# Keeping the last two chunks of h in SBUF, forming four more weight operands in place, and accumulating a product onto a PSUM copy of another

## The chip, the cores and the metric

One core of one Trainium2 chip runs the kernel. The metric is device time in microseconds of one launch. Of the kernel before, three runs are given. The profile is that of one more execution of the same program.

## What is computed

The reference adds two sublayers under a gate (batch 1, sequence S = 2048, D = 512, F = 1376, all float32):

```python
g = sigmoid((x * gate_w).sum(-1, keepdims=True))
a = x @ dft_hid_re.T ; b = x @ dft_hid_im.T
y = dft_seq_re @ a - dft_seq_im @ b          # Fourier mixing
h = silu(x @ w1) * (x @ w3)
out = g * y + (1 - g) * (h @ w2)
```

## The kernel before

**Arithmetic.** Every float32 operand of a matrix product is split into a high half, rounded to the type that TensorE takes (fp32r), and a low half, the rest. A product is then three matmuls (high by high, high by low, low by high), written by `mm3` (L79). `split` (L70) makes the halves: ScalarE copies the source into the high half (L71), VectorE subtracts that from the source for the low half (L74). On top of this every large product is computed by Strassen's scheme in Winograd's form: seven products of quarter blocks, P1 to P7, of operands that are first summed ("forms"), and sums of products in place of the eighth.

**Stages.** First come the hidden-dimension DFT (tiles `dP`, L190 to 240), whose result `ab` goes to DRAM, then the eleven column chunks c = 0 to 10 of h (`item`, L413; tiles `X`, `Y`, `Z`, `Yi`), and then the steps of the six output blocks (`step`, L847; tiles `P`, in the last third also `Lx`). Block b = (m, j): m = 0 is h @ w2, m = 1 and 2 are the two sequence DFTs, j is a half of the sequence. A step is one product (P1 ... P7) with one quarter q of its contraction: 12 matmuls, 6 where the quarter is half as wide. TensorE takes all of this in one stream.

**Order of the work.** The program is written in the order of the stages; a planner that simulates the engines at build time then orders each engine's instructions by priority, which is the order of the program, among what it takes to be ready. Each engine runs its list strictly in that order, so an instruction whose data are late holds back all that stand behind it on its engine. `keep_in_program_order` (called `pinned` in places) ties an instruction behind the one written before it on its engine; loads of the step stage are tied so (`fetch`, L580). DMAs are issued by SyncE (loads) and GpSimd (stores, and adds in DRAM). In the step stage `advance(n)` (L706) issues at step n the loads for step n + 8, the operand sums (L669) for step n + 4 and the halves for step n + 3.

**Buffers.** SBUF tiles come from pools with a fixed number of buffers: `f4` (19, float32 sources and results), `op` (28, operands that stay) and `zo` (8, halves that are used soon). A tile waits for a buffer that has fallen free. PSUM is held as four pairs of banks, `pp0` to `pp3`.

**h.** In `item`, `u2` and `u4` of chunk c end as two tiles of h, 128x1024 each; `store_h` (L409) writes them to DRAM: chunk 10 to `hpl`, the others to `hsp`. The first two output blocks (m = 0) load them again in `load_c` (L649), in pairs of chunks (q = 0, 1, 2; q = 2 is the single chunk 4 or 9), and chunk 10 in `load_plain` (L713), where the products with the last rows of w2 (the steps with q "pl") take it.

**Forms of the weights.** `forms(m, q, ks, keep)` (L473) loads two sources `r` from DRAM (L481), makes the sums `m..` (L490 to 501, L77), splits them, and either stores the halves to `fsp` (L514) or, with `keep`, leaves them in SBUF. The list `later` (L942 to 951) holds the forms made during the chunks, and `work` takes them off one by one, six for each chunk. For m = 1 the forms of P1, P5, P6 and P3 are made there for q = 0, 1, 2 and loaded again by `load_a`; those of q = 3 are made in place, two steps apart, from the third step of block 1 on (L1045 to 1049). The last entries of `later` are `inner_forms` (L530), which store to `lsp`.

**The end of a product.** At the last step of P1, P5 and P6, ScalarE copies the accumulated pair `whole` from PSUM to an `f4` tile (L904 to 906). P2 has a pair of its own; at its end VectorE adds it to the copy of P1 (L911), and `finish` (L779) scales by the gate, or stores.

**First chunks.** Before the loop over the chunks `first1(0)` and the parts of `second(0, n)` run in the order 0, 3, 1, 4, 2, 5; part 3 is the pinned copy of `X` to `Y` (L358). Then `prep_wa(1)` (L975) splits the weights of chunk 1, pinned too; chunk 1's first product (`first1(1)`, in chunk 0's `item`) takes them.

Of the kernel before, what the change touches and what calls it, by code (L numbers as in the profile page):

```python
# [12 lines left out]
P = 128  # L13
# [15 lines left out]
def fnet_swiglu_gate_kernel(  # L29
# [26 lines left out]
    def pair(k, name):  # L56
        return psum.tile([P, 2, 512], F32, tag=f"pp{k}", name=name)

    def raw(name, n=1024):
        return f4.tile([P, n], F32, tag="f4", name=name)  # L60

    def half(ap, n=2):
        return ap.rearrange("p (a n) -> p a n", a=n)
# [19 lines left out]

    ab = dram.tile([2, G, NQ, P, 2, 2, 256], F32, tag="ab", name="ab")
    hsp = dram.tile([G, 2, 2, NP, P, 512], F32, tag="hsp", name="hsp")
    hpl = dram.tile([G, 2, P, 512], F32, tag="hpl", name="hpl")
    gs = dram.tile([G, 2, 512], F32, tag="gs", name="gs")
    gsp = dram.tile([G, P, 1024], F32, tag="gsp", name="gsp")
    nbsp = dram.tile([G, 2, 2, P, 1024], F32, tag="nbsp", name="nbsp")
# [162 lines left out]
    def prep_wa(c):  # L252
        n = 768 if c == NC - 1 else 512
        if n == 512:
            t = zo.tile([P, 2, n], F32R, tag="zo", name=f"wa{c}")
            h, l = t[:, 0], t[:, 1]
        else:
            h, l = (zo.tile([P, n], F32R, tag="zo", name=f"wa{c}{v}") for v in "hl")
        split(h, l, WS[c][:, :n], c == 1)
        WA[c] = half(h, n // 256), half(l, n // 256)  # L260
# [82 lines left out]
                mm3(ps[:, g], w[0][:, k, sl], w[1][:, k, sl], xh[:, q], xl[:, q],  # L343
                    start and q == 0, q == 1, chain)

    X, S1, Y = {}, {}, {}

    def first1(c):
        X[c] = pair(c % 2, f"X{c}")
# [57 lines left out]
            WP.pop(i)  # L407

    def store_h(c, n, t):  # L409
        o = hpl[:, n] if c == NC - 1 else hsp[:, c // NP, n, c % NP]  # L410
        nc.gpsimd.dma_start(o.rearrange("g p n -> p g n"), half(t))

    def item(c, hooks):  # L413
# [59 lines left out]
    def forms(m, q, ks, keep):  # L473

        n = width(m, q)
        st = {}

        def load():
            for h, src in enumerate(rows_of(m, q)):
                st[h] = raw(f"r{m}{q}{h}")  # L480
                nc.sync.dma_start(st[h][:, : 2 * n], src[:, : 2 * n])  # L481
            st["a11"], st["a21"] = (st[0][:, v * n : (v + 1) * n] for v in range(2))
            st["a12"], st["a22"] = (st[1][:, v * n : (v + 1) * n] for v in range(2))

        def total(k):
            if k in ("P5", "P3") or k == "P7" and "m" not in st:
                st["m"] = raw(f"m{m}{q}{k}")
            if k == "P5":
                src = st["m"][:, :n]
                nc.vector.tensor_sub(src, st["a22"], st["a21"])  # L490
                st["s5"] = src
            elif k == "P6":
                src = st["m"][:, n : 2 * n]
                minus_sum(src, st["s5"], st["a11"])
                st["s6"] = src
            elif k == "P3":
                src = st["m"][:, :n]
                minus_sum(src, st["a12"], st["s6"])
            elif k == "P7":
                src = st["m"][:, n : 2 * n]  # L500
                nc.vector.tensor_sub(src, st["a11"], st["a21"])
            else:
                src = st[{"P1": "a11", "P2": "a12", "P4": "a22"}[k]]
            st[k] = src

        def parts(k):
            src = st[k]
            pool, tag = (op, "op") if keep else (f4, "f4")
            t = pool.tile([P, 2, n], F32R, tag=tag, name=f"f{m}{k}{q}")
            split(t[:, 0], t[:, 1], src)  # L510
            if keep:
                A[m, k, q] = t
            else:
                nc.gpsimd.dma_start(fsp[m, PRODS.index(k), q, :, : 2 * n], flat(t.bitcast(F32)))  # L514

        return ahead(load, total, parts, ks)
# [63 lines left out]
    def fetch(o, i):  # L580
        tc.keep_in_program_order(nc.sync.dma_start(o, i))

    def load_a(m, k, q):
        n = width(m, q)
        t = A[m, k, q] = op.tile([P, 2, n], F32R, tag="op", name=f"a{m}{k}{q}")
        fetch(flat(t.bitcast(F32)), fsp[m, PRODS.index(k), q, :, : 2 * n])
# [59 lines left out]
    def chunks(b, q):  # L646
        return width(BLOCKS[b][0], q) // 256

    def load_c(n):  # L649
        while LOADS and LOADS[0][0] <= n:  # L650
            _, b, k, q = LOADS.pop(0)
            w = chunks(b, q)
            r = RAW[b, k, q] = raw(f"{k}_{b}_{q}", w * 512)
            fetch(half(r, w), block(b, k, q))

# [55 lines left out]
    W2L, NGT, GT = {}, {}, {}  # L711

    def load_plain(b):  # L713
        t = raw(f"hp{b}")
        fetch(half(t), hpl[BLOCKS[b][1]].rearrange("n p f -> p n f"))
        PL[b] = {"n0": t[:, :512], "n1": t[:, 512:]}

    def prep_w2l():
        st = {}
# [127 lines left out]
    def step(n):  # L847
        b, k, q, form = STEPS[n]
        m, j = BLOCKS[b]
        if k[0] == "L":  # L850
            if q == 0 and k in ("LP7", "LP2"):
                load_other(LB[k == "LP2"], 0, 0)
            return inner(n)
        end = b == len(BLOCKS) - 1
        if q == 0:
            for f in ACTS.get((b, k), ()):
                f()
            if k in QUARTER:
                load_other(b, *QUARTER[k])
            if k in ("P1", "P5", "P2"):  # L860
                tag = {"P1": (1, 0)[b % 2], "P5": 2, "P2": 1 if end else 3}[k]
                WHOLE[k] = pair(tag, f"{k}_{b}")
                BANKS[k] = [WHOLE[k][:, r] for r in range(2)]
        acc = {"P6": "P1", "P7": "P1", "P4": "P1", "P3": "P5"}.get(k, k)
        ps, whole = BANKS[acc], WHOLE[acc]
        own = k in ("P1", "P5", "P2")
        fin = n == FINAL[b, k]
        zh, zl = ZO.pop(n)
        if q == "pl":
            e = QUARTER[k][0]  # L870
            for r in range(2):
                sl = slice(e * 256 + r * P, e * 256 + (r + 1) * P)
                mm3(ps[r], W2L[0][:, 0, sl], W2L[0][:, 1, sl], zh, zl, False, True, True)
        else:
            w = A[m, k, q]
            todo = [(q, w, zh, zl)]
            if n >= len(STEPS) - 2:
                LASTS.extend(todo)
                todo = LASTS if n == len(STEPS) - 1 else []
                if todo:  # L880
                    ps = [psum.tile([P, 512], F32, tag=f"pp{v}", name=f"last{v}") for v in (2, 3)]
            for r in range(2):
                for qq, ww, h, l in todo:
                    nch = chunks(b, qq)
                    for i in range(nch):
                        a = slice(i * 256 + r * P, i * 256 + (r + 1) * P)
                        c = slice(i * 512, (i + 1) * 512)
                        mm3(ps[r], ww[:, 0, a], ww[:, 1, a], h[:, c], l[:, c],
                            (own and qq == 0 or len(todo) == 2 and qq == todo[0][0]) and i == 0, (qq == NQS[m] - 1 or n == len(STEPS) - 3) and i == nch - 1, True)
                if n == len(STEPS) - 1:  # L890
                    finish(b, *QUARTER[k], U[k, b], ps[r], r)
        advance(n)
        for f in TASKS.pop(n, ()):
            f()
        if n == len(STEPS) - 3:
            U[k, b] = half(raw(f"u{k}_{b}"))
            finish(b, *QUARTER[k], U[k, b], whole)
        if not fin or n == len(STEPS) - 1:
            return
        if (k, b) in U:  # L900
            t = U[k, b]
            nc.vector.tensor_add(t[:, 0], t[:, 0], whole[:, 0])
            nc.scalar.activation(t[:, 1], whole[:, 1], AF.Copy)
        elif k in ("P1", "P5", "P6"):  # L904
            t = U[k, b] = half(raw(f"u{k}_{b}"))
            nc.scalar.activation(flat(t), flat(whole), AF.Copy)
        elif k == "P4":
            finish(b, *QUARTER[k], half(raw(f"u{k}_{b}")), whole)
        else:
            t = U[{"P3": "P6", "P7": "P5", "P2": "P1"}[k], b]  # L910
            nc.vector.tensor_add(flat(t), flat(t), flat(whole))  # L911
            finish(b, *QUARTER[k], t)

# [32 lines left out]
    later += prep_w2l()  # L946
    for q in range(3):
        later += forms(2, q, [k for k in PRODS if k != "P2"], False)
    for q in range(3):
        later += forms(1, q, ("P1", "P5", "P6", "P3"), False)  # L950
    later += inner_forms()

# [19 lines left out]
    first1(0)  # L972
    for n in (0, 3, 1, 4, 2, 5):
        second(0, n, 1)
    prep_wa(1)  # L975

    A0 = [(k, q) for k, _ in CHAIN for q in range(NQS[0])]
    for c in range(NC):
# [63 lines left out]
            TASKS.setdefault(start + 3 * q + max(i - 1, 0), []).append(f)  # L1042
    for i, (k, q) in enumerate(A0[8:]):
        TASKS.setdefault(int(1.25 * i), []).append(lambda k=k, q=q: load_a(0, k, q))
    todo = forms(1, 3, ("P1", "P5", "P6", "P3"), True)  # L1045
    todo[:2] = [lambda fs=todo[:2]: [f() for f in fs]]
    todo += [lambda k=k, q=q: load_a(1, k, q) for k, _ in CHAIN[:4] for q in range(3)]
    for i, f in enumerate(todo):
        TASKS.setdefault(AT[1, "P1", 0] + 2 + 2 * i, []).append(f)
    todo = forms(2, 3, [k for k in PRODS if k != "P2"], True)  # L1050
    todo[:2] = [lambda fs=todo[:2]: [f() for f in fs]]
    todo += [lambda k=k, q=q: load_a(2, k, q) for k in LORDER for q in range(3)]
# [75 lines left out]
```

## Time and profile before

| what | us |
|---|---|
| median of three runs | 704.97 (703.85, 704.97, 705.36) |
| the profiled execution's own time | 703.83 |
| its span in the trace | 701.9 |
| TensorE busy in the span | 695.6 |
| VectorE busy | 580.3 |
| ScalarE busy | 353.8 |

The span runs from the first to the last instruction of the program in the trace; 1.9 us of the execution's time lie outside of it. Times in the views are microseconds from the span's start. PE is TensorE, PEld its weight loads, DVE VectorE, ACT ScalarE, POOL GpSimd, SP SyncE. "Busy" of PE is the union of matmuls that overlap one another, so the share says little; starts of successive matmuls say more. In a row of the timeline, brackets hold how long the engine had been idle before it and what released it.

### The profile page before, as it was taken

What the parts mean: (1) busy time and instruction counts of PE and PEld (TensorE: products, weight loads), DVE (VectorE), ACT (ScalarE), POOL (GpSimd) and SP (SyncE); (2) the same over time, 40 slices, a digit from 0 to 9 for tenths busy, and PEclk for the clock granted to TensorE, in tenths of its full rate; (3) what the DMA queues carried; (4) which work ended last, traced back from release to release, by engine and by line L of the source; (5) the groups of instructions that cost most, each with busy time, mean ns of one, the idle gap of its engine ahead of it and who ended that gap; (6) DMA issues with size and microseconds to landing.
All of it is one profiled execution on the core that took longest, in us unless ns stands there. A gap on an engine that the chain in (4) does not pass through costs nothing.

```text
span 701.9 us, 8638 instructions
## 1 busy us (share of the span) xinstructions
PE 695.6 (99%) x3061; PEld 573.4 (82%) x3061; DVE 580.3 (83%) x650; ACT 353.8 (50%) x415; POOL 90.9 (13%) x144
## 2 busy tenths in 40 slices
PE   9999999999999999999999999999999999999997
PEld 7888878888888888788888888888888888888886
DVE  6999667597878987679988998679786966999886
ACT  6746356465555455373463464445534444544531
POOL 0012302131212222000000001000000020111110
PEclk9999999999999999999999999999999999999999
DMA  8387945677787989989569869930889979798823
GB/s 299 144 290 296 353 177 212 225 255 298 288 297 267 328 312 384 378 310 403 199 247 404 313 261 234 328 126 31 312 317 357 359 134 288 210 352 245 212 33 88
DMA packets 57451, 185.39 MB, mean 264 GB/s; under 512 B 6140, under 2 KB 6908, under 8 KB 57408
## 3 DMA queue, kind: packets, MB, share of 16 engines
q1 hardware_dynamic: 37008, 114.18, 45.6%
q0 software_dynamic: 20256, 70.53, 30.7%
q8 instruction: 24, 0.39, 0.2%
q14 instruction: 19, 0.16, 0.1%
q10 hardware_dynamic: 144, 0.13, 0.1%
HBM read 122.16 MB, written 62.66 MB: 263 GB/s over the span
## 4 chain that ended last, share of the span: by engine, by line
PE 94%; DMA 3%; DVE 2%; issue 1%; ACT 0%; DVEq 0%; SPq 0%; ACTq 0%
PE P L81 54%; PE X L81 15%; PE dP L81 10%; PE Z L81 7%; PE Lx L81 3%; PE Yi L81 2%; DMA B<-hsp 2%; PE Y L81 1%; PE dP L206 1%; PE last L81 1%; DMA dB<-head 0%; DVE u L439 0%; DVE B L669 0%; DVE s L405 0%; DVE u L435 0%
## 5 line engine op out<-in xcount | busy, mean ns | idle before, releaser
L71 ACT ACTIVATE zh<-B 128x1024 fp32r<-128x1024 f32 x146 | 148.3, 1019 | 176.3 <-PE P L81 145.1
L74 DVE TENSOR_TENSOR zl<-B,zh 128x1024 fp32r<-128x1024 f32 x146 | 169.6, 1169 | 41.2 <-ACT zh L71 36.0
L669 DVE TENSOR_TENSOR B<-B,B 128x1024 f32<-128x1024 f32 (+1 forms) x76 | 87.4, 1162 | 5.2 <-DMA B<-hsp 4.8
L81 PE MATMUL P<-zh,a2P 128*128 128x512 f32 x280 | 89.0, 389 | 0.0
L81 PE MATMUL P<-zh,a0P 128*128 128x512 f32 x280 | 87.5, 389 | 0.0
L81 PE MATMUL P<-zh,f1P 128*128 128x512 f32 x256 | 80.1, 389 | 0.0
L81 PEld LDWEIGHTS P<-zh,a0P 128*128 128x128 f32 x280 | 52.6, 188 | 11.0
L81 PEld LDWEIGHTS P<-zh,a2P 128*128 128x128 f32 x280 | 52.6, 188 | 10.9
L81 PE MATMUL P<-zh,a1P 128*128 128x512 f32 x192 | 60.4, 389 | 0.0
L81 PEld LDWEIGHTS P<-zh,f1P 128*128 128x128 f32 x256 | 48.0, 188 | 10.0
L81 PE MATMUL P<-zl,a0P 128*128 128x512 f32 x140 | 54.6, 390 | 0.7 <-DVE zl L74 0.7
L81 PE MATMUL P<-zl,a2P 128*128 128x512 f32 x140 | 54.5, 389 | 0.0
L81 PE MATMUL P<-zl,f1P 128*128 128x512 f32 x128 | 49.8, 389 | 0.0
L81 PEld LDWEIGHTS P<-zh,a1P 128*128 128x128 f32 x192 | 36.0, 188 | 7.6
L81 PE MATMUL P<-zl,a1P 128*128 128x512 f32 x96 | 37.3, 389 | 0.0
L81 PEld LDWEIGHTS P<-zl,a0P 128*128 128x128 f32 x140 | 26.3, 188 | 6.4 <-DVE zl L74 1.1
L81 PEld LDWEIGHTS P<-zl,a2P 128*128 128x128 f32 x140 | 26.3, 188 | 5.5
L81 PE MATMUL P<-zh,f2P 128*128 128x512 f32 x88 | 28.9, 389 | 0.0
L81 PEld LDWEIGHTS P<-zl,f1P 128*128 128x128 f32 x128 | 24.0, 188 | 5.0
L71 ACT ACTIVATE zh<-LB 128x1024 fp32r<-128x1024 f32 x14 | 14.9, 1063 | 20.4 <-PE P L81 18.2
L911 DVE TENSOR_TENSOR uP<-uP,P 128x1024 f32<-128x1024 f32 x16 | 19.5, 1219 | 4.4 <-PE P L81 4.3
L81 PEld LDWEIGHTS P<-zl,a1P 128*128 128x128 f32 x96 | 18.0, 188 | 3.7
(1137 smaller groups left out, 1476.0 us busy)
## 6 DMA issues: line engine op xcount, KB each, us to landing
B<-cc SPq DMA_DIRECT2D x56, 512.0 KB, 6.8
r<-ab SPq DMA_DIRECT2D x24, 512.0 KB, 6.3
hsp<-u POOLq DMA_DIRECT2D x20, 512.0 KB, 5.2
fsp<-f2P POOLq DMA_DIRECT2D x18, 512.0 KB, 4.0
a2P<-fsp SPq DMA_DIRECT2D x18, 512.0 KB, 7.2
B<-hsp SPq DMA_DIRECT2D x16, 512.0 KB, 10.4
fsp<-f0P POOLq DMA_DIRECT2D x14, 512.0 KB, 4.3
a0P<-fsp SPq DMA_DIRECT2D x14, 512.0 KB, 11.3
```

Of the source, the lines that this page charges most:

```text
L71: i = nc.scalar.activation(hi, src, AF.Copy)
L74: nc.vector.tensor_sub(lo, src, hi.bitcast(F32))
L81: nc.tensor.matmul(ps, u, v, start=first and n == 0, stop=last and n == 2, skip_group_check=chain)
L206: tc.keep_in_program_order(nc.tensor.matmul(ps[j][:, i], u[:, 0, sl], v[:, 0], start=start, stop=False, skip_group_check=True))
L669: nc.vector.tensor_add(t, t, RAW[b, o, q])
L911: nc.vector.tensor_add(flat(t), flat(t), flat(whole))
```

## The change

- **h of chunks 9 and 10 stays.** `store_h` keeps the tiles `u2` and `u4` of these chunks instead of storing them; `load_c` hands out the halves of chunk 9's tiles for the second-row blocks with q = 2, and `load_plain` those of chunk 10's. The DRAM tile `hpl` goes.
- **P2 onto the copy of P1.** In the blocks 0 to 3, P1 at its end is copied from its PSUM pair to pair 3, pinned, instead of to SBUF. P2 accumulates onto that copy, and `finish` reads the pair from PSUM; the addition on VectorE goes. In blocks 2 and 3 (m = 1) `finish` then copies the pair by ScalarE (L793).
- **Four more forms in place.** For m = 1 the forms of q = 2 leave the list `later`. Those of q = 3 are made in place in block 0, at steps 6, 8, 10 and 12, and those of q = 2 take their old place, steps 2, 4, 6 and 8 of block 1. Eight loads of stored forms follow, where there were twelve.
- **One split sooner.** `prep_wa(1)` moves from behind the parts of `second(0, ...)` to behind the second of them (part 3).

```diff
     def store_h(c, n, t):
-        o = hpl[:, n] if c == NC - 1 else hsp[:, c // NP, n, c % NP]
+        if c >= KEPT:
+            HL[c, n] = t
+            return
+        o = hsp[:, c // NP, n, c % NP]
...
             _, b, k, q = LOADS.pop(0)
+            m, j = BLOCKS[b]
             w = chunks(b, q)
+            if m == 0 and (c := (int(k[1]) - 1) * NP + 2 * q) >= KEPT:
+                RAW[b, k, q] = half(HL[c, int(k[2]) - 1])[:, j]
+                continue
...
     def load_plain(b):
-        t = raw(f"hp{b}")
-        fetch(half(t), hpl[BLOCKS[b][1]].rearrange("n p f -> p n f"))
-        PL[b] = {"n0": t[:, :512], "n1": t[:, 512:]}
+        j = BLOCKS[b][1]
+        PL[b] = {f"n{v}": half(HL[NC - 1, v])[:, j] for v in range(2)}
...
-            if k in ("P1", "P5", "P2"):
-                tag = {"P1": (1, 0)[b % 2], "P5": 2, "P2": 1 if end else 3}[k]
+            if k in ("P1", "P5"):
+                tag = {"P1": (1, 0)[b % 2], "P5": 2}[k]
...
-        own = k in ("P1", "P5", "P2")
+        own = k in ("P1", "P5")
...
+        elif k == "P1" and b not in LB:
+
+            WHOLE["P2"] = pair(3, f"P2_{b}")
+            BANKS["P2"] = [WHOLE["P2"][:, r] for r in range(2)]
+            pinned(nc.scalar.activation(flat(WHOLE["P2"]), flat(whole), AF.Copy))
...
-        elif k == "P4":
+        elif k in ("P2", "P4"):
             finish(b, *QUARTER[k], half(raw(f"u{k}_{b}")), whole)
         else:
-            t = U[{"P3": "P6", "P7": "P5", "P2": "P1"}[k], b]
+            t = U[{"P3": "P6", "P7": "P5"}[k], b]
...
-    for q in range(3):
+    for q in range(2):
         later += forms(1, q, ("P1", "P5", "P6", "P3"), False)
...
     for n in (0, 3, 1, 4, 2, 5):
         second(0, n, 1)
-    prep_wa(1)
+        if n == 3:
+            prep_wa(1)
...
-    todo = forms(1, 3, ("P1", "P5", "P6", "P3"), True)
-    todo[:2] = [lambda fs=todo[:2]: [f() for f in fs]]
-    todo += [lambda k=k, q=q: load_a(1, k, q) for k, _ in CHAIN[:4] for q in range(3)]
+    todo = []
+    for q in (3, 2):
+        fs = forms(1, q, ("P1", "P5", "P6", "P3"), True)
+        todo += [lambda fs=fs[:2]: [f() for f in fs]] + fs[2:]
+    todo += [lambda k=k, q=q: load_a(1, k, q) for k, _ in CHAIN[:4] for q in range(2)]
     for i, f in enumerate(todo):
-        TASKS.setdefault(AT[1, "P1", 0] + 2 + 2 * i, []).append(f)
+        TASKS.setdefault(AT[0, "P6", 0] + 2 * i if i < 4 else AT[1, "P1", 0] + 2 * i - 6, []).append(f)
```

More of the change, by code (lines that the diff above doesn't have):

```diff
@@ L85, in fnet_swiglu_gate_kernel @@
     hsp = dram.tile([G, 2, 2, NP, P, 512], F32, tag="hsp", name="hsp")
-    hpl = dram.tile([G, 2, P, 512], F32, tag="hpl", name="hpl")
     gs = dram.tile([G, 2, 512], F32, tag="gs", name="gs")
@@ L344, in prod @@
                     start and q == 0, q == 1, chain)
-    X, S1, Y = {}, {}, {}
+    KEPT = NC - 2
+    X, S1, Y, HL = {}, {}, {}, {}
     def first1(c):
```

## The prediction

> **What bounds the kernel now.** I read the page's busy shares first, then the chain, the windows, and last single rows of the timeline where a window shows too few matmuls.
>
> ```profile
> PE 695.6 (99%) x3061; PEld 573.4 (82%) x3061; DVE 580.3 (83%) x650; ACT 353.8 (50%) x415; POOL 90.9 (13%) x144
> ...
> 273.93 15.41 DMA B<-hsp
> ...
> 296.49 284.31 PE P L81 x1253
> ...
> 697.80 0.42 DVE uP L808
> ```
>
> A busy PE proves nothing, since its matmuls overlap; the pitch does. 284.31 us for 1253 matmuls are 0.227 a matmul. So from 296.5 to 580.8 PE runs at one pitch without a gap, and no part of the change touches the number of matmuls. What can be won is what PE loses against this pitch elsewhere. The windows count the matmuls in ten microseconds; at 0.227 there are room for 44 starts, and the count shows 45 or 46 with those begun before.
>
> ```profile
> core 0: us, PE busy (x) PEld busy (x) DVE busy (x) ACT busy (x) POOL busy (x), PEclk, DMA share, GB/s
> 90.00:100.00 10.00, 9.66 (x42) 7.32 (x42) 5.50 (x9) 6.46 (x10) 0.53 (x1) 1.00 0.27 106
> 270.00:280.00 10.00, 10.00 (x45) 8.28 (x45) 9.23 (x10) 6.95 (x7) 3.61 (x6) 1.00 1.03 417
> 280.00:290.00 10.00, 10.00 (x45) 8.26 (x44) 3.14 (x4) 2.97 (x4) 0.00 (x0) 1.00 0.99 394
> 290.00:300.00 10.00, 9.34 (x41) 7.43 (x40) 10.00 (x11) 3.44 (x5) 2.01 (x3) 1.00 0.95 345
> 300.00:310.00 10.00, 10.00 (x45) 8.26 (x44) 8.71 (x10) 7.78 (x9) 0.00 (x0) 1.00 0.80 273
> 310.00:320.00 10.00, 10.00 (x46) 8.28 (x45) 5.99 (x7) 7.46 (x9) 1.13 (x2) 1.00 1.03 399
> ```
>
> Two windows are short of three or four matmuls: 90 to 100 and 290 to 300. The PE rows give the sizes.
>
> ```profile
> 94.30 0.39 PE L81 MATMUL Z<-x1F3h,wb0l 128*128 128x512 f32 x1
> 95.02 0.50 PE L81 MATMUL X<-x0B11h,wa 128*128 128x512 f32 x1 [0.34 <-ACT wa L71]
> ...
> 96.55 0.40 PE L81 MATMUL X<-x0B11h,wa 128*128 128x512 f32 x1
> ```
> ```profile
> 295.22 0.61 PE L81 MATMUL P<-zh,a0P 128*128 128x512 f32 x2
> 296.49 0.50 PE L81 MATMUL P<-zl,a0P 128*128 128x512 f32 x1 [0.66 <-DVE zl L74]
> 296.83 0.39 PE L81 MATMUL P<-zh,a0P 128*128 128x512 f32 x1
> ```
>
> **Gap A**: from 94.30 to 96.55 PE starts six more matmuls in 2.25 us; at pitch it were 1.36, so 0.89 us are lost. **Gap B**: from 295.22 to 296.83 it starts three more in 1.61 us instead of 0.68: 0.93 us. What is left of the span besides is the first load and the tail behind PE's last matmul (from 697.8), and the change touches neither. So the prize is A + B = 1.82 us, 0.26% of the time, and it can't be more.
>
> **Part 1, the split sooner: gap A.**
>
> ```profile
> 86.62 1.03 ACT L358 ACTIVATE Y<-X 128x1024 f32<-128x1024 f32 x1
> 88.47 0.60 ACT L391 ACTIVATE s<-Yi 128x512 f32<-128x512 f32 x1 [0.83 <-PE Yi L81]
> ...
> 93.39 1.06 ACT L363 ACTIVATE s<-s 128x1024 f32<-128x1024 f32 x1 [1.95 <-DVE s L405]
> 94.36 0.61 ACT L71 ACTIVATE wa<-ws 128x512 fp32r<-128x512 f32 x1
> ```
> ```profile
> 89.10 0.69 DVE L392 TENSOR_TENSOR s<-s,Yi 128x512 f32<-128x512 f32 x1 [4.75 <-ACT s L391]
> 95.00 0.69 DVE L74 TENSOR_TENSOR wa<-ws,wa 128x512 fp32r<-128x512 f32 x1 [1.70 <-ACT wa L71]
> ```
> ```profile
> 51.91 0.70 SPq L250 DMA_DIRECT2D ws<-w  x1
> ```
>
> PE waits for `wa`, ScalarE's copy at 94.36, which stands behind the SiLU at 93.39 for no other reason than the order; its source was loaded at 51.9. Moved behind the copy of `Y`, it takes the 0.83 us that ScalarE is idle before 88.47 (0.61), and its low half (0.69) the 4.75 us that VectorE is idle before 89.10. Behind it on ScalarE stands L391, which starts no later as long as the source is there. Gain 0.89 us, cost nothing; were that idle stretch gone, L391 would be 0.61 late, and PE, which needs it next, as much.
>
> **Part 2, h stays: gap B.**
>
> ```profile
> 283.47 1.22 DVE L435 TENSOR_TENSOR u<-u,X 128x1024 f32<-128x1024 f32 x1 [2.08 <-PE X L81]
> 289.47 1.23 DVE L669 TENSOR_TENSOR B<-B,B 128x1024 f32<-128x1024 f32 x1 [4.78 <-DMA B<-hsp]
> ...
> 292.35 1.22 DVE L440 TENSOR_TENSOR u<-u,s 128x1024 f32<-128x1024 f32 x1
> ...
> 295.22 1.22 DVE L74 TENSOR_TENSOR zl<-B,zh 128x1024 fp32r<-128x1024 f32 x1
> ```
> ```profile
> 270.32 0.54 POOL L572 DMA_DIRECT2D lsp<-flP  x1 [5.40 <-DVE wu L77]
> ...
> 274.66 0.73 POOL L411 DMA_DIRECT2D hsp<-u  x1
> 275.38 0.56 POOL L572 DMA_DIRECT2D lsp<-flP  x1
> 278.40 0.72 POOL L411 DMA_DIRECT2D hsp<-u  x1 [2.45 <-DVE u L455]
> ```
>
> VectorE stood idle 4.78 us for the load of a block of h that took 15.41 us, then worked without a pause, and the low half that PE wants came at 296.44. That load (chunks 0 and 1 of the second row) stays in the change, but what it shares the DMA engines with goes: two stores of chunk 9 (274.66, 278.40), 0.52 MB each, and `lsp` stores like the two shown, which come five entries of `later` sooner (six go to a chunk, so most of a chunk, some 15 us). The engines moved 417 and 394 GB/s, their full share (1.03, 0.99). The two stores alone are 1.05 MB at 0.40 MB a microsecond, 2.6 us; with the two `lsp` stores 5.2 us. So the load lands 2.6 to 5.2 us sooner; I take 5.2, since both kinds leave this stretch. Gap B needs 0.93 of them, so it closes at both ends, and from 4.78 on VectorE doesn't wait at all. Were the load not moved at all, B would stay; that is the lower bound. Late next would be the same low half, now held by its own high half and by L669 work, 1.6 us ahead of PE by the lower end. The loads that go (two of chunk 10, four of chunk 9) and the stores of chunk 10 were not waited for by PE: cost and gain nothing. They need no sum; the tiles hold four of the 19 `f4` buffers to the end of block 1, but the two plain tiles, the loaded blocks and the copies of P1 held four there too.
>
> Whether the stores matter is where I weigh a rule. The Trainium skill, "DMA: Bandwidth & Descriptors", section "Issuing engines are not separate DMA queues", says that DMAs issued by different engines run interleaved on the same 16 DMA engines. By it the load profits from stores that another engine no longer issues, and the time is 703.1; were the load late only behind the eight loads that SyncE issued just ahead of it, B would stay and the time be 704.0, my first rival. The DMA share of 1.03 while both queues had work fits the rule; no row of this trace has the load without the stores.
>
> **Part 3, four more forms in place.**
>
> ```profile
> L74 DVE TENSOR_TENSOR f1P<-r,f1P 128x512 fp32r<-128x512 f32 x12 | 8.0, 684 | 3.8 <-ACT f1P L71 3.8
> L71 ACT ACTIVATE f1P<-r 128x512 fp32r<-128x512 f32 x12 | 7.1, 617 | 0.0
> L911 DVE TENSOR_TENSOR uP<-uP,P 128x1024 f32<-128x1024 f32 x16 | 19.5, 1219 | 4.4 <-PE P L81 4.3
> L906 ACT ACTIVATE uP<-P 128x1024 f32<-128x1024 f32 x17 | 17.2, 1010 | 1.8 <-PE P L81 1.8
> ```
>
> A set of four forms is seven half-width operations on VectorE (three sums, four low halves), 7 x 0.68 = 4.8 us, and four of 0.62 = 2.5 on ScalarE, with two loads `r`. One set moves from the chunks to block 1, where it takes the place of the other, so block 1 keeps its load; the other moves to block 0, steps 6 to 12, about 303 to 318. There VectorE is idle for 20 - 8.71 - 5.99 = 5.3 us in two windows and ScalarE for 4.8, and the 4.78 us of waiting come back as lead. It fits; without that idle time the low halves, some three steps ahead, would eat their lead first. Four stores to `fsp` and four loads go: only DMA time. Gain and cost on PE: nothing.
>
> **Part 4, P2 on the copy.** VectorE loses 4 x 1.22 = 4.9 us (L911), ScalarE gains 2 x 1.01 for blocks 2 and 3; the copy of P1 is 1.01 to SBUF and 1.03 to PSUM (`Y` above). None of it is in a gap. The pin adds a wait: in blocks 1 and 2 the copy of P1 stands behind a form's high half, and behind it all of ScalarE.
>
> ```profile
> 412.14 0.63 ACT L71 ACTIVATE f1P<-m11P 128x512 fp32r<-128x512 f32 x1 [0.87 <-DVE m11P L501]
> ...
> 417.44 0.39 PE L81 MATMUL P<-zh,a1P 128*128 128x512 f32 x1
> ```
>
> In block 2 that half is at 412.14, so the copy ends at 413.8; P6, which adds to the same pair, starts at 417.44: 3.6 us to spare. Its price is bounded below by nothing and above by how much later than 415.8 the half starts; I take nothing, the nearest row.
>
> **Sum.** 703.83 - 0.89 - 0.93 = 702.0 for the profiled execution. Its time lies 1.14 under the median of the runs (704.97), so the median becomes 704.97 - 1.82 = 703.15, say **703.1**.
>
> **Rivals.** (1) **One gap stays**, by the load that lands no sooner, or by ScalarE's `wa` still planned late: 704.97 - 0.9 = 704.1. For it: the load was ninth in SyncE's row. Against it: 0.93 us are little of 15.41. (2) **Nothing gained**, both stay or another small gap opens for them: 705.0. (3) **Slower: VectorE waits for another load.**
>
> ```profile
> r<-ab SPq DMA_DIRECT2D x24, 512.0 KB, 6.3
> ...
> a0P<-fsp SPq DMA_DIRECT2D x14, 512.0 KB, 11.3
> ```
> The planner took the load of h to land sooner than it did; it can err so again on `r`, now wanted in block 0, and set the first difference of it (L490) ahead of the low half of step 4. A buffer for it is free at the latest when L440 ends, 4.78 us sooner than 293.57, at 288.8. With 6.3 us to landing, the median of `r`, it is there at 295.1. Step 3 started with the second matmul of the row at 295.22, at 295.45; without gap B step 4 follows 12 matmuls later, at 298.2, and needs 0.6 and 1.2 us of VectorE before: the point is 296.4. At 11.3 us, the median of `a0P` loads in this stretch, it lands at 300.1, 3.7 late: 703.1 + 3.7 = 706.8. At 15.41 it is 7.8 late, 710.9. For it: gap B is this very thing. Against it: less traffic, and VectorE has other work there.
>
> **Chances.** Forecast 0.50, at 703.1, its own range 702.2 to 704.0; rival 1 0.19; rival 2 0.07; rival 3 0.24. A measurement here can tell about 0.2%, 1.4 us, from no change: faster is under 703.6, slower over 706.4. The forecast gives 0.44 to faster and 0.06 to same; rival 1 0.02 and 0.17; rival 2 all to same; rival 3 0.02 to same and 0.22 to slower. Together faster 0.46, same 0.32, slower 0.22. The range is 702.2 to 707.0: above it lies the worse half of rival 3, below it little.
>
> **What would show it.** Right: PE's wait for `wa` and for `zl` gone, 45 or 46 matmuls in both windows; VectorE's wait before L669 under 3 us; VectorE four instructions fewer, 646; ScalarE two more, 417; POOL eight fewer, 136. Wrong: a PE wait anywhere in blocks 0 to 2, with a DMA of `r` or a form's half ahead of it on VectorE or ScalarE; or L391 later than 88.6.

## The result, and the profile after

The changed kernel takes **703.06 us** (median of 22 runs, 702.00 to 705.38), the kernel before 704.88 (22 runs, 703.20 to 706.36): ratio 0.9973, 95% interval 0.9966 to 0.9981, 1.82 us less. That is the size that was forecast. The profiled execution is another matter: it took 703.77 us (span 701.7), only 0.06 less than the one before (703.83), and 0.7 more than its own median. So the traces have to show both, the two gaps that went and what took their place in this one execution.

The page's first line, with the instructions of each engine:

```profile
PE 695.5 (99%) x3061; PEld 574.1 (82%) x3061; DVE 575.8 (82%) x646; ACT 356.3 (51%) x417; POOL 85.5 (12%) x136
```

VectorE has four instructions fewer, ScalarE two more, GpSimd eight fewer, as counted beforehand. The windows, in the columns shown before:

```profile
90.00:100.00 10.00, 10.00 (x46) 8.19 (x45) 5.46 (x10) 6.61 (x9) 0.53 (x1) 1.00 0.38 150
230.00:240.00 10.00, 8.91 (x40) 7.06 (x39) 10.00 (x15) 4.13 (x6) 2.14 (x4) 1.00 0.90 322
270.00:280.00 10.00, 10.00 (x46) 8.27 (x45) 9.17 (x10) 6.95 (x7) 0.52 (x1) 1.00 0.98 342
280.00:290.00 10.00, 10.00 (x46) 8.29 (x45) 6.61 (x7) 2.36 (x3) 0.00 (x0) 1.00 0.82 320
290.00:300.00 10.00, 10.00 (x46) 8.28 (x45) 9.73 (x12) 7.04 (x8) 0.50 (x1) 1.00 0.55 188
```

The windows of both gaps hold 46 matmuls now (42 and 41 before). Around gap B the DMA engines moved 342, 320 and 188 GB/s, where it was 417, 394 and 345. A new window is short: 230 to 240, with 40.

**Gap A.** Rows of ScalarE, then of PE:

```profile
86.85 1.03 ACT L359 ACTIVATE Y<-X 128x1024 f32<-128x1024 f32 x1
87.79 0.63 ACT L71 ACTIVATE wa<-ws 128x512 fp32r<-128x512 f32 x1
88.73 0.60 ACT L392 ACTIVATE s<-Yi 128x512 f32<-128x512 f32 x1 [0.31 <-PE Yi L81]
```
```profile
94.55 0.39 PE L81 MATMUL Z<-x1F3h,wb0l 128*128 128x512 f32 x1
94.78 0.39 PE L81 MATMUL X<-x0B11h,wa 128*128 128x512 f32 x1
```

The split stands right behind the copy of `Y`, and PE goes from `Z` to `X` at pitch. ScalarE still idles 0.31 us for PE before its next copy, so that copy isn't late by the split.

**Gap B.** The first load of h of the second row (its tile's view), VectorE's row that used to wait for it, and the chain:

```profile
L585 SPq DMA_DIRECT2D B<-hsp x1: 457/457/457, 273.8 to 273.8; - x1
...
DMA to landing us min/median/max: 7.4/7.4/7.4
```
```profile
284.10 1.22 DVE L439 TENSOR_TENSOR u<-u,X 128x1024 f32<-128x1024 f32 x1 [3.39 <-PE X L81]
285.24 2.36 DVE L677 TENSOR_TENSOR B<-B,B 128x1024 f32<-128x1024 f32 x2
```
```profile
221.00 8.39 DMA fsp<-f1P
...
289.44 291.04 PE P L81 x1284
```

The load is issued when it was (273.8) and lands after 7.4 us instead of 15.41, at 281.2. The sum (L677, L669 before) follows L439 without a wait, and the chain stays on PE from 289.44 on for 1284 matmuls, 291 us, without a break.

**What took their place.** The chain now holds a store of `f1P` to `fsp`, near 230. Rows of PE and of VectorE:

```profile
231.23 0.39 PE L81 MATMUL X<-x1F1h,wb7l 128*128 128x512 f32 x1
232.71 0.50 PE L81 MATMUL Yi<-x1B21h,wp4zo 128*128 128x512 f32 x1 [1.09 <-DVE s L393]
```
```profile
229.42 0.43 DVE L265 TENSOR_TENSOR wu<-ws 128x256 f32<-128x256 f32 x1 [4.26 <-DMA fsp<-f1P]
```

PE starts `Yi` 1.48 us after its last matmul, 1.25 over the pitch, and some 0.1 more is lost right behind it: **loss in chunk 7**, 1.4 us. VectorE needs an `f4` buffer for the sums of chunk 8's weights, the buffer comes free when a store of `f1P` has landed, and `s`, which PE waits for, stands behind these sums. In the trace of before stands the same pair:

```profile
228.68 0.43 DVE L266 TENSOR_TENSOR wu<-ws 128x256 f32<-128x256 f32 x1 [2.83 <-DMA fsp<-f1P]
```

There VectorE waited 1.43 us less, and PE lost next to nothing. The change touches neither instruction. Whether it makes this loss, or chance does, no single pair of traces can tell.

### The profile page after: what moved, and what is told of

Its sections match the earlier page's. It is cut to its first block, busy times and chain, and to the rows that moved or that the text cites. A ratio compares the mean times of both kernels' runs of the same rounds, so it can differ in the third digit from the quotient of the medians.

```text
span 701.7 us, 8585 instructions
## 1 busy us (share of the span) xinstructions
PE 695.5 (99%) x3061; PEld 574.1 (82%) x3061; DVE 575.8 (82%) x646; ACT 356.3 (51%) x417; POOL 85.5 (12%) x136
## 4 chain that ended last, share of the span: by engine, by line
PE 91%; issue 5%; POOL 1%; DVE 1%; DMA 1%; DVEq 0%; POOLq 0%
PE P L81 55%; PE X L81 12%; PE dP L81 10%; PE Z L81 6%; PE Lx L81 3%; PE Yi L81 2%; DMA fsp<-f1P 1%; PE Y L81 1%; PE dP L205 1%; POOL fsp L518 1%; PE last L81 1%; PE wps L936 1%; POOL hsp L415 0%; DVE wu L77 0%; DVE s L353 0%
## 5 line engine op out<-in xcount | busy, mean ns | idle before, releaser
L71 ACT ACTIVATE zh<-B 128x1024 fp32r<-128x1024 f32 (+1 forms) x142 | 145.9, 1031 | 169.7 <-PE P L81 136.9
L74 DVE TENSOR_TENSOR zl<-B,zh 128x1024 fp32r<-128x1024 f32 (+1 forms) x142 | 167.1, 1183 | 45.9 <-ACT zh L71 39.0
L81 PE MATMUL P<-zh,f1P 128*128 128x512 f32 x320 | 99.9, 389 | 0.0
L677 DVE TENSOR_TENSOR B<-B,B 128x1024 f32<-128x1024 f32 (+1 forms) x70 | 83.6, 1204 | 1.2 <-DMA B<-cc 0.7
L81 PEld LDWEIGHTS P<-zh,f1P 128*128 128x128 f32 x320 | 60.1, 188 | 12.4
L81 PE MATMUL P<-zl,f1P 128*128 128x512 f32 x160 | 62.3, 389 | 0.0
L81 PE MATMUL P<-zh,a1P 128*128 128x512 f32 x128 | 40.7, 389 | 0.0
L81 PEld LDWEIGHTS P<-zh,a1P 128*128 128x128 f32 x128 | 24.0, 188 | 5.0
L81 PE MATMUL P<-zl,a1P 128*128 128x512 f32 x64 | 24.9, 389 | 0.0
L439 DVE TENSOR_TENSOR u<-u,X 128x1024 f32<-128x1024 f32 x11 | 13.4, 1218 | 10.6 <-PE X L81 10.3
L74 DVE TENSOR_TENSOR zl<-LB,zh 128x1024 fp32r<-128x1024 f32 x14 | 17.1, 1219 | 4.4 <-ACT zh L71 4.4
```

Source lines behind the costliest of these rows:

```text
L71: i = nc.scalar.activation(hi, src, AF.Copy)
L74: nc.vector.tensor_sub(lo, src, hi.bitcast(F32))
L81: nc.tensor.matmul(ps, u, v, start=first and n == 0, stop=last and n == 2, skip_group_check=chain)
L439: nc.vector.tensor_add(u4, u4, flat(x))
L677: nc.vector.tensor_add(t, t, RAW[b, o, q])
```

## The experiments

My theory: A is a matter of the place of one split alone; B is a load that lands late in proportion to what else the DMA engines carry, from whichever queue; the forms in place and P2 on the copy cost PE nothing; and the loss in chunk 7 varies from execution to execution. The rivals stand in the expectations. In all cases gaps are worked out from the starts of PE's rows against 0.227 us, and landings from the load's issue plus its time to landing.

**1. The kernel before, again.**

> The kernel before, once more, for the size of what varies between two executions of one program. Both gaps come back if the order of the instructions makes them: gap A 0.89 us (the wait of PE for wa near 95 us) and gap B near 296 us. Gap B hangs on one load's landing (289.35 in the first profile), so I expect it between 0.3 and 2 us. The loss in chunk 7 that the profile of the changed kernel shows (1.4 us near 232 us, a store of f1P to fsp that lands at 229.4) is put down by theory R (the landing of that store varies, in both kernels) to chance: this run may have it or not. By the rival C (the change makes it) this run has none.

705.26 us. Gap A 0.9, gap B 0.9, and in chunk 7:

```profile
232.38 0.39 PE L81 MATMUL X<-x1F1h,wb7l 128*128 128x512 f32 x1
233.51 0.50 PE L81 MATMUL Yi<-x1B21h,wp4zo 128*128 128x512 f32 x1 [0.74 <-DVE s L392]
```

A loss of 1.0 us in the kernel before: it isn't made by the change. Rival C falls.

**2. The changed kernel, again.**

> The changed kernel, once more. No gap near 95 us and none near 296 us; the first load of h of the second row (B<-hsp) lands between 280 and 285 us. Ratio to the kernel before 0.997 to 0.998. Chunk 7: by theory R (the landing of the store varies) the loss near 232 us has another size than 1.4 us, down to none; by rival C (made by the change) it is 1.2 to 1.6 us again.

702.68 us (12 runs), ratio 0.9971 (0.9958 to 0.9985). Neither gap; the load lands at 280.5; the loss in chunk 7 is 0.9 instead of 1.4.

**3. The split late again.**

```diff
-        if n == 3:
-            prep_wa(1)
+    prep_wa(1)
```

> The changed kernel with the split of chunk 1's weights back behind all parts of second(0, ...). Theory: gap A is made by this place alone, so PE waits 0.8 to 1.0 us for wa near 95 us again, gap B stays closed, and the time is 0.9 us over the changed kernel, 704.0. Rival (the planner would have put the split sooner anyway once other things move): no wait for wa, time as the changed kernel, 703.1.

703.56 us, ratio 0.9980 (0.9970 to 0.9990). PE waits as before:

```profile
93.72 0.39 PE L81 MATMUL Z<-x1F3h,wb0l 128*128 128x512 f32 x1
94.46 0.50 PE L81 MATMUL X<-x0B11h,wa 128*128 128x512 f32 x1 [0.36 <-ACT wa L71]
```

Gap A is back with 0.9 us, gap B stays shut. The median is 0.5 to 0.9 above the changed kernel's two medians; the intervals overlap, so the gap shows this better than the time does.

**4. h through DRAM again.**

```diff
...
-    KEPT = NC - 2
+    KEPT = NC
...
-        j = BLOCKS[b][1]
-        PL[b] = {f"n{v}": half(HL[NC - 1, v])[:, j] for v in range(2)}
+        t = raw(f"hp{b}")
+        fetch(half(t), hpl[BLOCKS[b][1]].rearrange("n p f -> p n f"))
+        PL[b] = {"n0": t[:, :512], "n1": t[:, 512:]}
```

> The changed kernel with h of chunks 9 and 10 stored to DRAM and loaded again. The prediction put gap B's end to the traffic beside the load: 2.6 us for the stores of chunk 9, 2.6 us for the stores to lsp that come sooner. By that theory the first load of h lands 2.6 us later than in the changed kernel, near 284, gap B stays closed (the load was at 289.35 with gap B of 0.93 us), and the time is 703.1. Rival H (the stores of h alone are what held the load): it lands near 289, gap B is back with 0.5 to 1.5 us, and the time is 704.0. Rival F (the forms alone): it lands near 281 and nothing changes.

702.93 us, ratio 0.9969 (0.9958 to 0.9979). The stores of h beside the load, and the load:

```profile
L416 POOL DMA_DIRECT2D hsp<-u x2: 724/732/741, 273.0 to 278.2; - x2
```
```profile
L586 SPq DMA_DIRECT2D B<-hsp x1: 384/384/384, 273.3 to 273.3; - x1
...
DMA to landing us min/median/max: 9.9/9.9/9.9
```

Landing at 283.1, 2.6 later than in run 2 (280.5), and gap B shut; the landing near 289 of rival H did not come, nor that near 281 of rival F. This is the load with and without the two stores, 9.9 against 7.4 and 7.6 us.

**5. The forms as before.** The list for m = 1 gets q = 2 back, and block 1 has q = 3 alone.

```diff
-    for q in range(2):
+    for q in range(3):
         later += forms(1, q, ("P1", "P5", "P6", "P3"), False)
...
```

> The changed kernel with the forms as before (q = 2 stored during the chunks, q = 3 in block 1). With h stored again and the forms changed, the load of h of the second row landed 2.6 us later than in the changed kernel, which leaves some 6 us of the 8 us for the stores to lsp that come sooner with the forms. By this theory (the traffic adds up) the load lands near 286.5 here, gap B, which needs a landing by about 288.4, stays closed, and the time is that of the changed kernel, 702.9. Rival F (only the forms close B): it lands near 289 and B is back with 0.5 to 1.5 us, 703.8.

703.48 us, ratio 0.9972 (0.9959 to 0.9985).

```profile
L585 SPq DMA_DIRECT2D B<-hsp x1: 371/371/371, 273.8 to 273.8; - x1
...
  DVE B L677: 2.0, 1
...
DMA to landing us min/median/max: 12.6/12.6/12.6
```

Landing at 286.4; VectorE waits 2.0 us for it, PE not at all: gap B is shut without the forms too. Rival F falls.

**6. P2 in a pair of its own.**

```diff
-            if k in ("P1", "P5"):
+            if k in ("P1", "P5", "P2"):
...
-            pinned(nc.scalar.activation(flat(WHOLE["P2"]), flat(whole), AF.Copy))
...
```

> The changed kernel with P2 in a pair of its own and added to P1's copy by VectorE, as before. Theory: four VectorE additions of 1.22 us more and two ScalarE copies fewer, none on the path; gaps A and B stay closed, and the time is that of the changed kernel within 0.2%, 702.9. Rival (the additions hold back the halves): a wait of PE for zl or zh in blocks 0 to 3 of up to 1.2 us each, 703.5 to 706.

702.69 us (10 runs), ratio 0.9961 (0.9947 to 0.9976), beside run 5 with 0.9972 on the same chip. No wait of PE in the blocks 0 to 3. P2 on the copy neither gains nor costs anything that these runs can tell.

**7 to 9. One part alone, added to the kernel before:** h kept; the forms in place; the split sooner. Each is its part of the change's diff, of which these lines are the core:

```diff
+    KEPT = NC - 2
...
-    for q in range(3):
+    for q in range(2):
         later += forms(1, q, ("P1", "P5", "P6", "P3"), False)
...
-    prep_wa(1)
+        if n == 3:
+            prep_wa(1)
```

> The kernel before with h of chunks 9 and 10 kept and nothing else. Theory: the load of h of the second row lands 2 to 3 us sooner than in the kernel before, near 287; gap B closes or is under 0.2 us, and gap A stays, 0.9 us. Rival F (only the forms close B): landing 289 to 291, gap B 0.9 us or more.

> The kernel before with the four forms of q = 2 in place and nothing else. Theory: the load of h of the second row lands near 283, as in the changed kernel with h stored again; gap B closed, gap A stays, 0.9 us. Rival H (the stores of h hold the load): near 289, gap B 0.9 us.

> The kernel before with the split of chunk 1's weights behind part 3 and nothing else. Theory: no wait of PE for wa near 95 us, gap B back with 0.5 to 1.5 us since its load still lands near 289 to 291.

One run each: 702.61, 703.49 and 703.16 us. The 22 runs of the changed kernel spread over 3.4 us, so three single times rank nothing; what counts here is the traces. For the same reason it stays open what gap B alone is worth in time: of all kernels only the last of these has gap A shut and gap B open. The load in the three, in this order, with VectorE's wait where there is one:

```profile
L584 SPq DMA_DIRECT2D B<-hsp x1: 370/370/370, 273.7 to 273.7; - x1
...
  DVE B L676: 2.3, 1
...
DMA to landing us min/median/max: 13.0/13.0/13.0
```
```profile
L581 SPq DMA_DIRECT2D B<-hsp x1: 487/487/487, 273.6 to 273.6; - x1
...
DMA to landing us min/median/max: 9.0/9.0/9.0
```
```profile
L581 SPq DMA_DIRECT2D B<-hsp x1: 371/371/371, 273.3 to 273.3; - x1
...
  DVE B L669: 4.6, 1
...
DMA to landing us min/median/max: 15.2/15.2/15.2
```

13.0 us with h kept, 9.0 with the forms moved, 15.2 with neither. Gap B is shut in the first two and gap A open (0.9); in the third it is the other way round:

```profile
294.45 0.61 PE L81 MATMUL P<-zh,a0P 128*128 128x512 f32 x2
295.57 0.50 PE L81 MATMUL P<-zl,a0P 128*128 128x512 f32 x1 [0.51 <-DVE zl L74]
```

Against 15.4 us in the kernel before, h alone takes 2.4 and the forms alone 6.4; both together take 8.0 in the changed kernel. The two shares nearly add up, and either shuts a gap of 0.93. (The third load landed at 288.4, a little ahead of the 289 to 291 that I had expected.)

**10. The loss in chunk 7 taken away.** `item` calls five functions, h0 to h4, at fixed places of a chunk (its hooks). In the changed kernel, the sums of chunk 8's weights move from h1 to h2 of chunk 7:

```diff
-            if c + 1 < NC:
+            if c + 1 < NC and c != 7:
                 prep_wb(c + 1)
...
         def h2(c=c):
+            if c == 7:
+                prep_wb(c + 1)
             work(1)
```

> The changed kernel with the sums of chunk 8's weights, whose buffer hangs on the store of f1P, one hook later in chunk 7. The loss in chunk 7 so far: 0.01, 1.37, 1.13, 0.88, 0.27 and 0.01 us in six profiles (kernel before, changed, before, changed, split late, h stored), a mean of 0.6. Theory R: it is the wait of VectorE for the store's landing ahead of work that PE needs; moved behind that work it is under 0.1 us in this profile whatever the landing, and the time is 0.3 to 0.9 us under the changed kernel, 702.2. Rival: the sums are then late for chunk 8's own weights, PE waits there instead, and the time is that of the changed kernel or up to 1 us over it.

701.94 us (6 runs), ratio 0.9953 (0.9937 to 0.9969). The store took 8.07 us here, and yet, on VectorE and on PE:

```profile
230.17 0.68 DVE L393 TENSOR_TENSOR s<-s,Yi 128x512 f32<-128x512 f32 x1
230.77 0.42 DVE L265 TENSOR_TENSOR wu<-ws 128x256 f32<-128x256 f32 x1
```
```profile
230.97 0.39 PE L81 MATMUL X<-x1F1h,wb7l 128*128 128x512 f32 x1
231.19 0.39 PE L81 MATMUL Yi<-x1B21h,wp4zo 128*128 128x512 f32 x1
```

`s` stands ahead of the sums now, PE runs through, and no wait for chunk 8's weights opens. So the loss is that wait. The other profiles bear it out: in all eleven with the sums in their old place the loss is what this store took to land less 7.0 us, to within 0.03, and next to nothing where it took 7.0 or less (8.39 us and a loss of 1.39, 8.05 and 1.03, 7.30 and 0.29, 6.94 and 0.02).

**11 and 12. The same edit in the kernel before, and once more in the changed kernel, side by side.**

> The kernel before with the sums of chunk 8's weights one hook later in chunk 7, as in the changed kernel with that edit. It takes the varying loss in chunk 7 out of both, so that the two gaps stand alone. Theory: loss in chunk 7 under 0.05 us, gap A 0.9, gap B 0.9; time 0 to 0.6 us under the kernel before, and 1.8 us over the changed kernel with the same edit. Rival G (a part of gap A is given back in chunk 7: in the five profiles with A shut and nothing else late before it the loss was 1.37, 0.89, 1.01, 0.92 and 0.32, in the five with A open 0.03, 1.02, 0.28, 0.14 and 0.23): the edit is worth 0.3 here and 0.9 in the changed kernel, so the two are 2.4 us apart.

> The changed kernel with the sums of chunk 8's weights one hook later, once more and beside the kernel before with that edit. No gap near 95, 232 or 296 us. Theory: 1.8 us under the kernel before with the same edit, ratio to the kernel before 0.995 to 0.997, time near 702.0. Rival G: 2.4 us under it.

In the kernel before it is worth nothing: 704.90 us beside 704.92, ratio 0.9994 (0.9984 to 1.0003). In the changed kernel 702.47, ratio 0.9966 (0.9952 to 0.9980). They are 2.4 us apart, with 12 runs each that spread over 2.0 and 3.3 us. Loss in chunk 7 is nil in both profiles. But gap B of the kernel before is larger than it ever was, 1.4 instead of 0.9; its load, and PE:

```profile
L581 SPq DMA_DIRECT2D B<-hsp x1: 370/370/370, 273.1 to 273.1; - x1
...
  DVE B L669: 5.2, 1
...
DMA to landing us min/median/max: 16.0/16.0/16.0
```
```profile
294.55 0.61 PE L81 MATMUL P<-zh,a0P 128*128 128x512 f32 x2
296.26 0.50 PE L81 MATMUL P<-zl,a0P 128*128 128x512 f32 x1 [1.10 <-DVE zl L74]
```

In the first profile of before, PE stood at the same place at 295.22 and the load landed at 289.35. Here PE is 0.67 sooner, the load is issued 0.8 sooner, and it lands at 289.1, only 0.2 sooner. So in this profile most of what PE gained upstream went into gap B. The two gaps add up to 2.3 us here, and that, not a give-back in chunk 7, is most of what the two profiles have apart (spans 701.7 and 699.1 us). Rival G isn't excluded by it, but it isn't borne out either. It put the edit at 0.3 us here and 0.9 in the changed kernel; it brought 0.0 here, and there 0.2 to 1.1, by which medians one takes. And the store landed after 7.9 us in the profile here, with gap A open, and after 8.1 and 6.9 in runs 10 and 12, with A shut; less 7.0, that would have been a loss of 0.9, 1.1 and none. (With the sums moved the next store goes out some 3 us sooner, so these three need not be the same as the eleven.)

All profiles together (us; landing of the load of h, the three losses of PE, median and count of runs):

| kernel | landing | gap A | chunk 7 | gap B | median |
|---|---|---|---|---|---|
| before, first profile | 289.4 | 0.9 | 0.0 | 0.9 | 704.88 (22) |
| before, again | 290.8 | 0.9 | 1.0 | 0.9 | 705.26 (1) |
| changed, first profile | 281.2 | 0 | 1.4 | 0 | 703.06 (22) |
| changed, again | 280.5 | 0 | 0.9 | 0 | 702.68 (12) |
| changed, split late | 280.6 | 0.9 | 0.3 | 0 | 703.56 (12) |
| changed, h through DRAM | 283.1 | 0 | 0.0 | 0 | 702.93 (12) |
| changed, forms as before | 286.4 | 0 | 1.0 | 0 | 703.48 (12) |
| changed, P2 in its own pair | 280.2 | 0 | 0.9 | 0 | 702.69 (10) |
| before, only h | 286.8 | 0.9 | 0.1 | 0 | 702.61 (1) |
| before, only forms | 282.6 | 0.9 | 0.2 | 0 | 703.49 (1) |
| before, only split | 288.4 | 0 | 0.3 | 0.8 | 703.16 (1) |
| before, sums later | 289.1 | 0.9 | 0 | 1.4 | 704.90 (12) |
| changed, sums later | 279.8; 279.4 | 0; 0 | 0; 0 | 0; 0 | 701.94 (6); 702.47 (12) |

Smaller waits that come and go are left out of the table. In "before, again" they add up to some 1.2 us, near 30, 66 and 85 us; "before, only forms" has 0.5 each near 66 and 85; "changed, h through DRAM" has 0.6 near 31 and 0.9 at 85.3, where PE waits for ScalarE's copy `dt1P` (L226). So the 0.0 of that row in chunk 7 came behind another loss of the size of gap A.

The last row is the best version seen. Against the kernel before it is clearly faster; against the changed kernel its intervals overlap, so what is shown is that the loss is gone from its profiles, and a gain of some 0.5 us is likely but not proven.

## Why the prediction was right, and where it wasn't

**Gap A** was read rightly. The row that was to tell, L391 "later than 88.6", now starts at 88.73; the whole execution ran 0.25 behind by then (94.55 against 94.30 for the last `Z` matmul ahead of the gap), and the row itself waits for PE. The mark should have been the wait, not the clock.

**Gap B** closed for the reason given, traffic beside the load, but its term was mis-sized. The step put the load 2.6 to 5.2 us sooner, and it came 8.0 sooner. The half that is due to h held (2.6 forecast; 2.4 measured by adding it alone, 2.3 to 2.4 by taking it back). The other half, the forms, was put at 2.6 too, and measured 6.4 by adding them alone and 5.0 to 5.2 by taking them back. It counted "the two `lsp` stores" that I had quoted. A third stood between the quoted rows:

```profile
271.16 0.53 POOL L572 DMA_DIRECT2D lsp<-flP  x1 [0.29 <-DVE flP L74]
```

The tile's view of before, and that of the changed kernel, show how many leave:

```profile
L572 POOL DMA_DIRECT2D lsp<-flP x5: 534/543/562, 261.2 to 275.4; - x5
```
```profile
L576 POOL DMA_DIRECT2D lsp<-flP x3: 532/541/562, 255.4 to 259.9; - x3
```

Five `lsp` stores that were issued between 261 and 276 are issued before 260 now. Two of them had landed when the load was issued; the other three, 1.57 MB, landed while it was under way. And SyncE's own queue was shorter: of its loads 3.67 MB landed between the issue and the landing of this one (its own 0.52 included), and 2.88 MB in the changed kernel. The term missed one of three stores, and these loads altogether. From the load's issue to its landing the DMA engines are full in each of the four kernels (share 1.00 to 1.03). By their rate over that time they moved 6.2 MB before (403 GB/s), 5.3 with h alone kept (410), 3.0 with the forms alone moved (338) and 2.6 in the changed kernel (350). Why the rate is lower in the last two, no run here shows. The sum didn't change by the missed size, since either half is more than the 0.93 us that were wanted.

**The rule weighed.** The Trainium skill, "DMA: Bandwidth & Descriptors", section "Issuing engines are not separate DMA queues", says that DMAs of different issuing engines share the same engines. The runs agree: with h alone kept (run 7) the same 3.67 MB of SyncE's loads land beside this load as before, only GpSimd's two stores of h are gone, and it took 13.0 us instead of 15.4. So it wasn't late behind the loads of its own engine alone, as rival 1 had it; the 0.79 MB by which these were fewer with the forms moved had a part in the rest.

**Forms in place.** Nothing on PE, as forecast. Rival 3 put a wait for `r` ahead of step 4's low half, with the load issued at 288.8. The view of tile `r` in block 0:

```profile
L485 SPq DMA_DIRECT2D r<-ab x2: 382/557/732, 294.9 to 295.4; - x2
...
L494 DVE TENSOR_TENSOR m13P<-r,r x1: 690/690/690, 314.2 to 314.2; 128x512 f32<-128x512 f32 x1
...
DMA to landing us min/median/max: 6.7/7.1/7.5
```

The loads are issued 6 us later than I allowed, and the first difference of them stands at 314.2, 11 us behind the landing. The rival's place was wrong, not only its odds.

**P2 on the copy.** In block 2, rows of ScalarE and PE:

```profile
409.95 0.61 ACT L71 ACTIVATE f1P<-m11P 128x512 fp32r<-128x512 f32 x1
410.47 1.00 ACT L915 ACTIVATE P<-P 128x1024 f32<-128x1024 f32 x1
```
```profile
417.12 0.39 PE L81 MATMUL P<-zh,a1P 128*128 128x512 f32 x1
```

The copy is done at 411.5, and the step for which I had reserved it starts at 417.1: 5.7 us to spare, where I had worked out 3.6.

**The sum.** 1.82 forecast, 1.82 measured between medians. The size was right; that the two agree to the hundredth is luck, as the interval of the ratio reaches from 1.3 to 2.4 us. For the profiled execution the sum gave 702.0, and it came 703.77. Between the two profiled executions it didn't show: 1.85 gained in A and B, 1.35 more lost in chunk 7, 0.25 more before 94 us, leaves 0.25, and the spans differ by 0.26 (701.93 to 701.67). One step of the argument failed here without harm. I wrote that besides A and B only the first load and the tail are lost, and so that 1.82 is all that there is. That was true of the one execution I had. The next execution of the same kernel lost 1.0 us in chunk 7 and some 1.2 in smaller waits, and with the sums later gap B was 1.4. My baseline for the median (704.97) held such losses, and as far as these profiles tell the forecast was right because they stay in the changed kernel, too. How much of them stays is open: with gap A shut and sums not moved the loss in chunk 7 was 1.4, 0.9, 0.0, 1.0, 0.9 and 0.3, with it open 0.0, 1.0, 0.3, 0.1 and 0.2. That looks like a part of gap A given back; eleven profiles that overlap so far don't show it, and since the loss follows the landing of one store, the change would have to make that landing later, which was not shown.

## What to carry to other kernels

When a load lands late, count all the bytes that every queue moves between its issue and its landing, not the ones in sight, and ask of each part of a change how many of them it takes away: here two parts each sufficed alone. A wait on a store that frees a buffer, placed ahead of work that TensorE needs, is a loss that comes and goes with the landing; look for it in rows where an engine already waits for a DMA (2.83 us here) with no harm yet, and move the waiting instruction behind the urgent one. Read two profiles of the kernel before naming a prize below one microsecond.

## What the runs showed of the hardware

A load that is issued sooner need not land sooner: 273.93 to 289.35 in one execution of the kernel before, 273.1 to 289.1 with the sums later. And the same store of 512 KB, at the same place of the program, took 6.96 us to land in one execution of the kernel before and 8.05 in another, with the same order of instructions. PE lost next to nothing there in the first and 1.0 us in the second. What makes the difference was not found.
